# RetNet block and squared-ReLU FFN on one core: chunks 11 to 39 turned off TensorE, w_out converted by pairs of pieces from block 1 on

## The chip, the cores and the metric

One core of a Trainium2 chip runs the whole kernel. Its engines work side by side, each through its own queue in order: TensorE (PE, and PEld for its weight loads), VectorE (DVE), ScalarE (ACT), GpSimd (POOL) and the queue on SyncE (SP) that issues nearly all DMAs. The metric is the time of one execution on the device in microseconds, as the median of several runs.

## The reference

Eight heads of retention over 8 sequences of 576 tokens, then an FFN over all 4608 tokens:

```python
scores = scale * np.matmul(q, k.transpose(0, 1, 3, 2))
Dmat = np.where(rel >= 0, gamma[:, None, None] ** rel[None, :, :], 0.0)
ret = scores * Dmat[None, :, :, :]
attn = np.matmul(ret, v).astype(np.float32)          # (8, 8, 576, 64)
x = attn.transpose(0, 2, 1, 3).reshape(4608, 512)
h = np.maximum(x @ w_in, 0.0)                        # w_in 512 x 2048
out = (h * h @ w_out).astype(np.float32)             # w_out 2048 x 512
```

q, k and v are float32. The two weights reach the kernel as 64-bit words (float64), so it converts them to float32 itself with integer operations.

## The kernel before

**Phases.** In the first phase the kernel computes the retention and, interleaved with it, g = relu(x w_in)^2. In the second phase it multiplies g by w_out. Both products are done by the Strassen-Winograd scheme of seven products (`PRODUCTS`), the sums of quarters being made on VectorE. g goes to DRAM (`g_dram`) in five of its seven forms (`G_KEPT`); the other two, S2 and S4, are made in the second phase by `made`, from forms that have come back. This is the same in both kernels.

**Retention.** There are 40 chunks: four of 128 tokens and a half one of 64 for each sequence (chunks 4, 9, 14 and so on are half). For each chunk q and k must be turned, so that the head's dimension lies on partitions. `turn` (L406) does it on TensorE: sixteen small matmuls against an identity (eight for a half chunk) into PSUM (L414), and two copies out, k by ScalarE (L417) and q by VectorE (L418). The second way is `flip` and `spread`: two VectorE transposes of 32x32 blocks (L392), one for k and one for q, and sixteen ScalarE copies of 32x256 slices, eight for a half chunk (L403), which `move` issues a few at a time. Before the change chunks 0 to 10 and 19 to 39 are turned by TensorE, and chunks 11 to 18 in the second way. `scores` multiplies k by q (L435) and masks the product on VectorE (L443). `retain_a`, `retain_b` and `retain_c` sum up the chunk before: the products within the chunk (L457), the state's growth (L460) and the state's part (L492). A small ScalarE copy of x_ps (L495) is written at the end of `retain_b`, and since it reads the PSUM tile that L457 of `retain_c` writes next, TensorE waits for it. The result is copied into xT by ScalarE (L514).

**xT.** A block is 512 tokens; there are nine. `xT[n]` holds block n's input until its steps are done. Two rooms are in `room`; block 2 has a third one in W[6], and a rule in `retain_c` (L511) issues what is left of an old block before its room is overwritten.

**Steps.** The FFN's input side is a list of steps. Block 0 has 16 of its own kind (L578) while w_in is being converted; each of blocks 1 to 8 has 28 steps, 4 pairs of row blocks (mp) times 7 products (j), of eight 128x256 matmuls each (L614). j = 0 is followed by a ScalarE copy (L624), j = 1 and 2 by a VectorE add each (L626, L628), j = 3 by a ScalarE activation (L630) and a square on POOL (L631), and j = 4, 5 and 6 by a VectorE add and a square each (L633, L637, L640, L621). PSUM has three banks for them. One iteration of the main loop (L739) handles one chunk: `retain_a`, `turn`, `move`, some steps (`ffn(.., 0)`, the first half), `retain_b`, `scores`, `retain_c`, and steps again (`ffn(.., 1)`, the second half). `PACE` says how many steps must be done by which token, so the order is fixed when the kernel is built.

**w_out.** The weights of the second phase are converted in 16 pieces of 128x512 words. A piece takes five parts (`w_out_parts`): `one` and `two` on VectorE (L210, L214), with `two` two ScalarE activations (L218, L219, together `beside`), then `three`, `four` and `five` on VectorE (L222, L225, L228), `three` needing the activations. After every second piece come two parts of sums (L245 to L248), after every fourth eight more and two stores to DRAM. With three fetches in front these are 139 parts. A step of a block issues one part at most: before the change 13 of them in the first steps of block 1, and one in every step from block 3 on. `held` keeps a part with activations out of the last step of a first half. The pieces arrive by DMA through the SP queue in three rooms, and the fetch of piece j+3 is issued by the last part of piece j. Its staging area is W[5] and the beginning of W[6].

Of the kernel before, what the change touches and what calls it, by code (L numbers as in the profile page):

```python
# [15 lines left out]
C = 128  # L16
# [24 lines left out]
def kernel(  # L41
# [152 lines left out]
    def fetch_w(j):  # L194
        if j < len(pieces) and wide:
            nc.sync.dma_start(raw_of(j).bitcast(I64).rearrange("p (c f) -> p c f", c=N_DM), piece_src(j))
# [53 lines left out]
    def w_out_parts():  # L250

        for j in range(N_W1, N_W1 + 3):
            yield lambda j=j: fetch_w(j)
        for j in range(N_W1, len(pieces)):
            one, two, beside, three, four, five = round_parts(j)
            yield one
            yield two, beside
            yield three
            yield four

            def last(j=j, five=five):
                five()
                fetch_w(j + 3)

            yield last
            wi, m, e = pieces[j]
            mh, mq = divmod(m, N_MQ)
            if e == 1:

                at = slice(2 * mh, 2 * mh + 2)  # L270
                b = [stage[0][:, o, at, :] for o in range(4)] + [stage[1][:, o, at, :] for o in range(3)]
                r1, r2, r3, r4 = right_sums(*b)
                yield lambda r1=r1, r2=r2: (r1(), r2())
                yield lambda r3=r3, r4=r4: (r3(), r4())
            if e == 1 and mh == 1:

                for st_, at in ((stage[0], slice(0, 4)), (stage[1], slice(4, 7))):
                    yield from right_sums(*(st_[:, :, o, :] for o in range(NP)))
                    yield lambda st_=st_, at=at, mq=mq: nc.sync.dma_start(
                        w2_dram[at, :, mq, :].rearrange("o p f -> p o f"), st_.rearrange("p o s f -> p o (s f)"))  # L280
# [63 lines left out]

    st = {i: {} for i in range(N_CH)}
    u_ps = [None]

    xT = {n: xT_room[n % 2 if n < 2 else (n - 3) % 2] for n in range(N_BLK)}
    xT[2] = W[6][:, 0:N_DM * TOK].rearrange("p (c t) -> p c t", c=N_DM)

# [24 lines left out]

    N_TURN, N_BACK = 11, 19  # L380
    moves = []

    def new_qk(i):
        t = work3.tile([128, 2, HP, C], F32, tag="qk", name="qk")
        st[i]["qT"], st[i]["kT"] = t[:, 0, :, :], t[:, 1, :, :]
        return t

    def flip(i):
        cs = chunks[i][3]
        t = st[i]["flip"] = work2.tile([128, 4, 2, HP, 32], F32, tag="flip", name="flip")  # L390
        for j in (1, 0):
            nc.vector.transpose(t[:cs, :, j, :, :], loaded[i][j][:cs].rearrange("s (p e) (d a) -> s (e d) p a", e=2, d=2))  # L392

    def spread(i):
        t, to = st[i]["flip"], new_qk(i)
        for b in range(chunks[i][3] // 32):
            for g in range(4):
                moves.append((i, to[32 * g:32 * g + 32, :, :, 32 * b:32 * b + 32], t[32 * b:32 * b + 32, g, :, :, :]))

    def move(count, i=N_CH):  # L400

        while moves and count and moves[0][0] <= i:
            nc.scalar.copy(*moves.pop(0)[1:])  # L403
            count -= 1

    def turn(i):  # L406
# [90 lines left out]
    def retain_c(i):  # L497

        b_, ci, c0, cs = chunks[i]
        own, grow = within(i, 0)  # L500
        more = ci + 1 < NCH
        for j in range(0, len(own), 2):
            for f in own[j:j + 2] + (grow[j:j + 2] if more else []):
                f()
        tok = b_ * S + c0
        at = tok
        p = xp[0][:, :, 0:256].rearrange("p a (g t) -> p a g t", g=2)
        while at < tok + cs:
            n = at // TOK

            while steps and steps[0][0] <= (n - 2 if n > 4 else n - 3):  # L511
                step()
            end = min(tok + cs, (n + 1) * TOK)
            nc.scalar.copy(xT[n][:, :, at - n * TOK:end - n * TOK].rearrange("p (a g) t -> p a g t", a=2),  # L514
                           p[:, :, :, at - tok:end - tok])
            if more and at == tok:
                grown(i, 1)
            at = end
            if n_next[0] < N_BLK and (n_next[0] + 1) * TOK <= at:
                steps.extend(block_steps(n_next[0]))  # L520
                n_next[0] += 1
        st[i] = loaded[i] = None
# [76 lines left out]
    def ffn_in(n, mp, j):  # L599

        if j == 0 and mp == 0:

            if n not in sums_x:
                sums_x[n] = sum_x(n)
            for f in sums_x[n]:
                f()
        left, right, to = PRODUCTS[j]
        if j in OPENS:
            sums[to] = ps_f.tile([128, 2, HT], F32, tag="f", name=f"h_{to}")
        p = sums[to]  # L610
        for mm in range(2):
            w = w_in[mp][:, mm, WI_SLOT[left], :, :]
            for c in range(2):
                nc.tensor.matmul(p[:, mm, :], lhsT=w[:, c, :], rhs=xs[n][right][:, c, :],  # L614
                                 start=(j in OPENS and mm == 0 and c == 0), stop=(j in CLOSES and c == 1),
                                 skip_group_check=True)
        g = g_of(mp)
        p1, u2, p15 = (p_room[mp % 2][:, s, :, :] for s in range(3))

        def square(t):  # L620
            nc.vector.scalar_tensor_tensor(t, t, 0.0, t, op0=ALU.max, op1=ALU.mult)  # L621

        if j == 0:
            nc.scalar.copy(p1, p)  # L624
        elif j == 1:
            nc.vector.tensor_tensor(u2, p, p1, op=ALU.add)  # L626
        elif j == 2:
            nc.vector.tensor_tensor(p15, p, p1, op=ALU.add)  # L628
        elif j == 3:
            nc.scalar.activation(g["A11"], p, AF.Relu)  # L630
            nc.gpsimd.tensor_tensor(g["A11"], g["A11"], g["A11"], op=ALU.mult)  # L631
        elif j == 4:
            nc.vector.tensor_tensor(g["A22"], p, p15, op=ALU.add)  # L633
            square(g["A22"])
        elif j == 5:

            nc.vector.tensor_tensor(g["S3"], p, u2, op=ALU.add)  # L637
            square(g["S3"])
        else:
            nc.vector.tensor_tensor(g["A12"], p, p1, op=ALU.add)  # L640
            square(g["A12"])
            queue.extend(g_sums(n, mp))

        if mp == N_MP - 1 and j in (3, 4, 5) and n_next[0] > n + 1:
            if n + 1 not in sums_x:
                sums_x[n + 1] = sum_x(n + 1)
            sums_x[n + 1].pop(0)()
        if j in (6, 0, 1, 2, 3):
            some(2 if n == 1 and mp == 0 else 1)
        if n == 1 and 1 <= j < 5 and mp + 1 < N_MP:  # L650
            sums_w.setdefault(mp + 1, sum_w_in(mp + 1)).pop(0)()

        if n >= 3 or n_w2[0] < 3 + 2 * 5:
            if not (held[0] and type(w_out_next[0]) is tuple):
                n_w2[0] += 1
                f = w_out_next[0]
                w_out_next[0] = next(w_out_steps, None)
                for f in f if type(f) is tuple else (f,):
                    f and f()
            if n == N_BLK - 2 and (mp, j) in ((2, 3), (3, 3)):  # L660
                assert w_out_next[0] is None
                fetch_w2(mp - 2)
# [34 lines left out]
    def ffn(i, half):  # L697

        gone[0] += chunks[max(0, min(i, N_CH - 1))][3] / 2
        if steps and steps[0][0] == 0:  # L700

            move(6)
            for f in (step, lambda: convert(6)) if half else (lambda: convert(6), step):
                f()
            if half and steps and steps[0][0] == 0:
                step()
                convert(6)
            return
        if not behind:
            behind.append((gone[0] - HALF, done[0]))  # L710
        points = behind + [p for p in PACE if p[0] > behind[0][0]]
        want = points[-1][1]
        for (x0, y0), (x1, y1) in zip(points, points[1:]):
            if gone[0] < x1:
                want = y0 + (y1 - y0) * (gone[0] - x0) / (x1 - x0)
                break
        count = max(1, int(want) - done[0])
        while steps and count:
            held[0] = half == 0 and count == 1
            move(3)  # L720
            step()
            count -= 1
        held[0] = False
# [15 lines left out]
    for i in range(N_CH + 1):  # L739
# [42 lines left out]
        else:  # L782
            if i == N_EARLY + 1:
                gone[0] = TOK
            retain_a(i - 1)
            if i < N_TURN or N_BACK <= i < N_CH:
                turn(i)
            move(C, i)
            ffn(i - 1, 0)
# [1 line left out]
            if i < N_CH:  # L791
                scores(i)
            retain_c(i - 1)
            if N_TURN <= i + 1 < N_BACK:
                spread(i + 1)
            if N_TURN <= i + 2 < N_BACK:
                flip(i + 2)
            ffn(i - 1, 1)
        if i == 0:
# [267 lines left out]
```

## Time and profile before

| what | value |
|---|---|
| median of 7 runs | 985.08 us (984.05 to 986.17) |
| profiled execution, its own time | 985.45 us |
| profiled execution, span from first to last instruction | 983.6 us |
| mean granted TensorE clock | 0.998 |
| first phase, block 0 begins its last step | 102.4 us |
| first phase, retention of the last chunk | about 529 us |
| second phase begins | about 585 us |
| DMA | 181.46 MB, mean 184 GB/s |

| stretch, us | PE busy | DVE busy | ACT busy | POOL busy |
|---|---|---|---|---|
| 0 to 101.8 | 93.0 | 74.9 | 45.4 | 26.9 |
| 101.8 to 230 | 127.9 | 96.2 | 74.1 | 31.5 |
| 230 to 515 | 282.8 | 223.7 | 73.3 | 60.8 |
| 515 to 584.7 | 69.3 | 44.2 | 8.1 | 7.5 |
| 584.7 to 983.6 | 395.2 | 321.0 | 33.4 | 0.0 |

In the prediction's extracts a line of the timeline gives the start in us, the length in us, the engine (a "q" behind it means the engine's sequencer), the line of the kernel, the operation, the tile written and the tiles read, the number of instructions run together, and in brackets the idle time before and what ended it. A line of the groups gives busy time, mean duration in ns, and idle time before with its releaser. [...]

### The profile page before, as it was taken

To read this page: it belongs to the slowest core of one execution; us is meant where nothing else is said; L and a number is where in the kernel's file an instruction comes from. 1 tells how busy PE (TensorE), PEld (TensorE's weight loads), DVE (VectorE), ACT (ScalarE), POOL (GpSimd) and SP (SyncE) were. 2 spreads that over 40 slices of the span, in tenths; PEclk is the share of its full clock that TensorE was granted. 3 is DMA by queue.
4 is the path that set the end of the run, shared out by engine and by line. 5 is a ranking of instruction groups with operands and counts; after the bars stand their busy time and mean duration, and the time that the engine had idled before them with its cause. 6 is when DMAs were issued, how large, how long until landed. Compare 5 with 4: busy or idle time off the path is not lost.

```text
span 983.6 us, 24277 instructions
## 1 busy us (share of the span) xinstructions
PE 968.1 (98%) x10404; PEld 864.1 (88%) x10404; DVE 760.0 (77%) x1426; ACT 234.2 (24%) x573; POOL 126.7 (13%) x121
## 2 busy tenths in 40 slices
PE   7899999999999999999999999999999999999998
PEld 6645788888888888888888899999999999999998
DVE  3889798648777877878776577878888788787876
ACT  3554474752223222312211010000000000000000
POOL 3221222311213221221201000000000000000000
PEclk9999999999999999999999999999999999999999
DMA  8985665643756676585348966645352544534241
GB/s 201 244 224 151 178 189 138 175 141 90 259 188 192 163 276 191 162 285 144 127 182 303 355 247 239 225 162 196 109 204 109 182 180 165 208 124 172 86 172 44
DMA packets 172012, 181.46 MB, mean 184 GB/s; under 512 B 118144, under 2 KB 132480, under 8 KB 165248
## 3 DMA queue, kind: packets, MB, share of 16 engines
q1 hardware_dynamic: 169792, 179.38, 56.4%
q8 instruction: 82, 1.34, 0.6%
q10 hardware_dynamic: 2112, 0.52, 0.3%
q14 instruction: 26, 0.21, 0.1%
HBM read 109.36 MB, written 70.52 MB: 183 GB/s over the span
## 4 chain that ended last, share of the span: by engine, by line
PE 87%; DVE 8%; DMA 2%; ACT 1%; issue 1%; SPq 0%; DVEq 0%; ACTq 0%
PE o_b L916 16%; PE h_b L614 15%; PE o_a L916 11%; PE o_c L916 11%; PE h_a L614 10%; PE h_c L614 10%; PE h_ps L578 4%; PE x_ps L457 3%; PE sc_ps L435 2%; PE x_ps L492 2%; PE t_ps L414 2%; DMA g<-g_dram 1%; DVE room L621 1%; DVE w L222 1%; DVE w L225 1%
## 5 line engine op out<-in xcount | busy, mean ns | idle before, releaser
L614 PE MATMUL h_b<-room,w 128*128 128x256 f32 x736 | 177.2, 384 | 1.2 <-DVE room L541 1.0
L614 PEld LDWEIGHTS h_b<-room,w 128*128 128x128 f32 x736 | 137.4, 190 | 21.2 <-PE t_ps L414 1.1
L916 PE MATMUL o_b<-w,room 128*128 128x128 f32 x1168 | 144.4, 276 | 0.2 <-DVE room L868 0.2
L916 PEld LDWEIGHTS o_b<-w,room 128*128 128x128 f32 x1168 | 137.3, 192 | 0.4 <-DVE room L868 0.4
L916 PE MATMUL o_c<-w,room 128*128 128x128 f32 x1008 | 123.0, 275 | 0.0
L916 PEld LDWEIGHTS o_c<-w,room 128*128 128x128 f32 x1008 | 117.7, 192 | 0.0
L614 PE MATMUL h_c<-room,w 128*128 128x256 f32 x480 | 114.4, 381 | 0.0
L614 PE MATMUL h_a<-room,w 128*128 128x256 f32 x448 | 107.5, 383 | 0.0
L614 PEld LDWEIGHTS h_c<-room,w 128*128 128x128 f32 x480 | 90.7, 190 | 12.3
L614 PEld LDWEIGHTS h_a<-room,w 128*128 128x128 f32 x448 | 84.0, 190 | 11.6
L916 PE MATMUL o_a<-w,a 128*128 128x128 f32 x688 | 85.7, 276 | 0.0
L916 PEld LDWEIGHTS o_a<-w,a 128*128 128x128 f32 x688 | 81.2, 192 | 0.1
L631 POOL TENSOR_TENSOR room<-room 128x512 f32<-128x512 f32 x32 | 34.0, 1061 | 365.9 <-ACT room L630 295.1
L930 ACT COPY r<-o_a 128x128 f32<-128x128 f32 x53 | 14.2, 267 | 272.5 <-PE o_a L916 236.8
L621 DVE SCALAR_TENSOR_TENSOR room<-room 128x512 f32<-128x512 f32 x96 | 70.3, 732 | 3.3
L633 DVE TENSOR_TENSOR room<-h_b,room 128x512 f32<-128x512 f32 x32 | 22.1, 690 | 50.9 <-PE h_b L614 47.4
L578 PE MATMUL h_ps<-room,w 128*128 128x512 f32 (+1 forms) x152 | 59.8, 542 | 1.5 <-DVE w L228 0.8
L375 POOL TENSOR_TENSOR q_ld<-q_ld,dv 128x512 f32<-128x512 f32 (+1 forms) x39 | 47.2, 1211 | 75.2 <-DMA q_ld<-in_q_dram 64.5
L457 PEld LDWEIGHTS x_ps<-qk,v_ld 64*64 64x64 f32 x1152 | 40.5, 137 | 13.8 <-issue 11.8
L457 PE MATMUL x_ps<-qk,v_ld 64*64 64x64 f32 x1152 | 49.9, 227 | 1.4 <-ACT u_sb L495 1.3
L578 PEld LDWEIGHTS h_ps<-room,w 128*128 128x128 f32 x152 | 28.3, 195 | 24.4 <-issue 20.5
L403 ACT COPY qk<-flip 32x256 f32<-32x256 f32 x120 | 48.3, 402 | 1.7
(115 smaller groups left out, 1435.2 us busy)
## 6 DMA issues: line engine op xcount, KB each, us to landing
g_dram<-room SPq DMA_DIRECT2D x32, 1280.0 KB, 5.8
a<-g_dram SPq DMA_DIRECT2D x30, 1024.0 KB, 6.0
room<-g_dram SPq DMA_DIRECT2D x15, 1024.0 KB, 6.3
w<-w_dram SPq DMA_DIRECT2D x7, 1792.0 KB, 10.6
out_dram<-room SPq DMA_DIRECT2D x17, 512.0 KB, 3.3
w<-in_moe_w_in_dram SPq DMA_DIRECT2D x16, 512.0 KB, 5.7
w<-in_moe_w_out_dram SPq DMA_DIRECT2D x16, 512.0 KB, 5.2
v_ld<-in_v_dram SPq DMA_DIRECT2D x31, 256.0 KB, 3.5
```

Source lines behind the costliest of these rows:

```text
L375: engine.tensor_tensor(t, t, dv[:cs, :, NCH + ci:NCH + ci + 1].to_broadcast([cs, H, D]), op=ALU.mult)
L403: nc.scalar.copy(*moves.pop(0)[1:])
L414: nc.tensor.transpose(p[:, h, j, hp, :], loaded[i][j][rows(h), 2 * hp:2 * hp + 2, :], ident[rows(h), rows(h)])
L435: nc.tensor.matmul(sc[e][rows(h), hp, :], lhsT=kT[rows(e), hp, t], rhs=qT[rows(e), hp, t], start=True, stop=True, skip_group_check=True)
L457: own.append(lambda hp=hp, e=e, b=b: nc.tensor.matmul(x_at(hp, b, h), lhsT=s["vs"][rows(h), 2 * hp + b, :], rhs=s["ret"][rows(h), e, hp, : ...
L492: nc.tensor.matmul(x_at(hp, b, h), lhsT=u[rows(e), hp, :], rhs=s["qT"][rows(e), hp, CH * h:CH * h + CH], start=clears(b, hp // 2), stop=Fa ...
L578: nc.tensor.matmul(p.rearrange("p h t -> p (h t)"), lhsT=w[:, c, :], rhs=xT[0][:, c, lo * HT:hi * HT], start=(c == 0), stop=(c == N_DM - 1))
L614: nc.tensor.matmul(p[:, mm, :], lhsT=w[:, c, :], rhs=xs[n][right][:, c, :], start=(j in OPENS and mm == 0 and c == 0), stop=(j in CLOSES a ...
L621: nc.vector.scalar_tensor_tensor(t, t, 0.0, t, op0=ALU.max, op1=ALU.mult)
L631: nc.gpsimd.tensor_tensor(g["A11"], g["A11"], g["A11"], op=ALU.mult)
L633: nc.vector.tensor_tensor(g["A22"], p, p15, op=ALU.add)
L916: nc.tensor.matmul(p, lhsT=s["lefts"][left][:, m, :], rhs=w_out[j][:, m, WO_SLOT[right], :], start=(i in OPENS and m == 0), stop=(i in CLO ...
```

## The change

- `w_out_parts` handles two pieces together: `one`, `two` with `beside` for the first and the second piece, then `three`, `four`, `five` for the first and for the second.
- A part of w_out is issued by a step while fewer than 0.8 x (steps done since block 0) have been issued. So the conversion begins with block 1 and ends early in block 7.
- All blocks use the two rooms for xT by turns; block 2 no longer lies in W[6]. The rule at L511 is the same for all blocks.
- `N_BACK` is gone: every chunk from 11 on goes by `flip`. `spread` is merged into it. The two transposes become two entries of a list `flips`, of which `ffn` issues one before each step. The slices carry the number of steps at which they become due, three after the second transpose, and `move` issues none before that unless it is called with C, as it is at the start of an iteration for the chunk that is needed next.

```diff
--- before.py
+++ after.py
@@ -251,18 +251,21 @@
 
         for j in range(N_W1, N_W1 + 3):
             yield lambda j=j: fetch_w(j)
-        for j in range(N_W1, len(pieces)):
-            one, two, beside, three, four, five = round_parts(j)
-            yield one
-            yield two, beside
-            yield three
-            yield four
-
-            def last(j=j, five=five):
-                five()
-                fetch_w(j + 3)
-
-            yield last
+        for j in range(N_W1 + 1, len(pieces), 2):
+
+            pair = [round_parts(j - 1), round_parts(j)]
+            for one, two, beside, *_ in pair:
+                yield one
+                yield two, beside
+            for i, (_, _, _, three, four, five) in zip((j - 1, j), pair):
+                yield three
+                yield four
+
+                def last(i=i, five=five):
+                    five()
+                    fetch_w(i + 3)
+
+                yield last
             wi, m, e = pieces[j]
             mh, mq = divmod(m, N_MQ)
             if e == 1:
@@ -344,9 +347,7 @@
 
     st = {i: {} for i in range(N_CH)}
     u_ps = [None]
-
-    xT = {n: xT_room[n % 2 if n < 2 else (n - 3) % 2] for n in range(N_BLK)}
-    xT[2] = W[6][:, 0:N_DM * TOK].rearrange("p (c t) -> p c t", c=N_DM)
+    xT = {n: xT_room[1 - n % 2] for n in range(N_BLK)}
 
 
 
@@ -377,7 +378,7 @@
 
 
 
-    N_TURN, N_BACK = 11, 19
+    N_TURN = 11
     moves = []
 
     def new_qk(i):
@@ -385,22 +386,29 @@
         st[i]["qT"], st[i]["kT"] = t[:, 0, :, :], t[:, 1, :, :]
         return t
 
+    flips = []
+
     def flip(i):
         cs = chunks[i][3]
-        t = st[i]["flip"] = work2.tile([128, 4, 2, HP, 32], F32, tag="flip", name="flip")
-        for j in (1, 0):
+        t = work2.tile([128, 4, 2, HP, 32], F32, tag="flip", name="flip")
+
+        def one(j):
             nc.vector.transpose(t[:cs, :, j, :, :], loaded[i][j][:cs].rearrange("s (p e) (d a) -> s (e d) p a", e=2, d=2))
 
-    def spread(i):
-        t, to = st[i]["flip"], new_qk(i)
-        for b in range(chunks[i][3] // 32):
-            for g in range(4):
-                moves.append((i, to[32 * g:32 * g + 32, :, :, 32 * b:32 * b + 32], t[32 * b:32 * b + 32, g, :, :, :]))
+        def two():
+            one(0)
+            to = new_qk(i)
+            for b in range(cs // 32):
+                for g in range(4):
+
+                    moves.append((i, done[0] + 3, to[32 * g:32 * g + 32, :, :, 32 * b:32 * b + 32], t[32 * b:32 * b + 32, g, :, :, :]))
+
+        flips.extend([lambda: one(1), two])
 
     def move(count, i=N_CH):
 
-        while moves and count and moves[0][0] <= i:
-            nc.scalar.copy(*moves.pop(0)[1:])
+        while moves and count and moves[0][0] <= i and (moves[0][1] <= done[0] or count == C):
+            nc.scalar.copy(*moves.pop(0)[2:])
             count -= 1
 
     def turn(i):
@@ -508,7 +516,7 @@
         while at < tok + cs:
             n = at // TOK
 
-            while steps and steps[0][0] <= (n - 2 if n > 4 else n - 3):
+            while steps and steps[0][0] <= n - 2:
                 step()
             end = min(tok + cs, (n + 1) * TOK)
             nc.scalar.copy(xT[n][:, :, at - n * TOK:end - n * TOK].rearrange("p (a g) t -> p a g t", a=2),
@@ -650,7 +658,7 @@
         if n == 1 and 1 <= j < 5 and mp + 1 < N_MP:
             sums_w.setdefault(mp + 1, sum_w_in(mp + 1)).pop(0)()
 
-        if n >= 3 or n_w2[0] < 3 + 2 * 5:
+        if n_w2[0] < 0.8 * (done[0] - N_0):
             if not (held[0] and type(w_out_next[0]) is tuple):
                 n_w2[0] += 1
                 f = w_out_next[0]
@@ -718,6 +726,9 @@
         while steps and count:
             held[0] = half == 0 and count == 1
             move(3)
+            for f in flips[:1]:
+                f()
+            del flips[:1]
             step()
             count -= 1
         held[0] = False
@@ -783,7 +794,7 @@
             if i == N_EARLY + 1:
                 gone[0] = TOK
             retain_a(i - 1)
-            if i < N_TURN or N_BACK <= i < N_CH:
+            if i < N_TURN:
                 turn(i)
             move(C, i)
             ffn(i - 1, 0)
@@ -791,9 +802,7 @@
             if i < N_CH:
                 scores(i)
             retain_c(i - 1)
-            if N_TURN <= i + 1 < N_BACK:
-                spread(i + 1)
-            if N_TURN <= i + 2 < N_BACK:
+            if N_TURN <= i + 2 < N_CH:
                 flip(i + 2)
             ffn(i - 1, 1)
         if i == 0:
```

## The prediction

> **What bounds the kernel now.** I read the busy table first, then the waits of the matrix engine, then its weight loads in order of time around a turn, then the loads of the other engines by stretch.
>
> ```profile
> PE 968.1 (98%) x10404; PEld 864.1 (88%) x10404; DVE 760.0 (77%) x1426; ACT 234.2 (24%) x573; POOL 126.7 (13%) x121
> ```
>
> TensorE is busy 98% of the span, and its longest listed wait for another engine in the stretch from 230 to 535 us is 1.1 us. In the first phase one step of a block (eight 128x256 matmuls) goes out every 1.72 us with hardly a break, so an instruction taken off TensorE's queue there shortens the kernel by its place in the queue, not by its latency. That place is read from the weight loads. The first two views are a chunk that TensorE turns, and one of the chunks (11 to 18) that VectorE and ScalarE turn already:
>
> ```profile
> 407.54 0.14 PEld L460 LDWEIGHTS u_ps<-v_ld,k_ld 64*64 64x64 f32 x2
> 407.75 0.32 PEld L414 LDWEIGHTS t_ps<-w,k_ld 64*128 64x128 f32 x8
> 408.00 0.33 PEld L414 LDWEIGHTS t_ps<-w,q_ld 64*128 64x128 f32 x8
> 408.39 0.73 PEld L614 LDWEIGHTS h_b<-room,w 128*128 128x128 f32 x4
> ```
>
> ```profile
> 160.63 0.14 PEld L460 LDWEIGHTS u_ps<-v_ld,k_ld 64*64 64x64 f32 x2
> 160.84 0.30 PEld L614 LDWEIGHTS h_b<-room,w 128*128 128x128 f32 x2
> ```
>
> After the last L460, the next step's weights follow in 0.21 us without a turn and in 0.85 us with one: a turn holds TensorE for 0.64 us (407.75 to 408.39), though its sixteen matmuls are listed at 223 ns each.
>
> ScalarE has room; VectorE has it in most places, but not at the beginning of block 1:
>
> ```profile
> 110.00:130.00 20.00, 20.00 (x251) 17.07 (x250) 17.85 (x28) 12.94 (x32) 4.11 (x3) 1.00 0.75 230
> 130.00:150.00 20.00, 19.81 (x236) 16.50 (x236) 19.72 (x28) 15.19 (x36) 7.93 (x6) 1.00 0.70 187
> ...
> 170.00:190.00 20.00, 20.00 (x209) 17.02 (x211) 12.22 (x19) 15.84 (x40) 5.07 (x4) 1.00 0.72 203
> ```
>
> The columns are stretch, length, then PE, PEld, DVE, ACT and POOL busy. From 130 to 150 VectorE works 19.7 of 20 us. ScalarE, carrying the slices of chunks 11 to 18, stands at 13 to 16 of 20. Between 230 and 515 it is busy only 73 of 285 us.
>
> **What goes.** Chunks 19 to 39 lose their turn: 21 x 0.64 = 13.4 us of TensorE's queue (half chunks show 0.64 too). Four of the 21 turns (chunks 20, 25, 30, 35) come when the chunk before is a half one and L476 returns at once, so they stand alone between two runs of steps. A run of three steps takes 5.38 us, one of four 7.10: beyond 1.72 a step each run costs 0.21. Merging four pairs of runs gives 4 x 0.2 = 0.8 us. And two waits of the scores for L418's copy out of PSUM, 0.9 and 0.3 (1.1 listed from 230 to 535), have no cause any more. Sum: 13.4 + 0.8 + 1.1 = **15.3 us**. Beyond 585 us (the second phase, 399 us) nothing changes: its `made` sums stand in both kernels.
>
> **What comes on ScalarE.** Sixteen full and five half chunks bring 16x16 + 5x8 = 296 slices (L403):
>
> ```profile
> L403 ACT COPY qk<-flip x120: 400/402/405, 114.3 to 214.7; 32x256 f32<-32x256 f32 x120
> ```
>
> 296 x 0.402 = 119 us, less 21 copies L417 of 0.54 = 11. So 73 + 108 = 181 of some 270 us: two thirds, which is hidden on average. It isn't hidden at one place per chunk. L495, a tiny copy of x_ps, stands in ScalarE's queue behind the first half's steps, and TensorE's retain_c (L457) waits for it. Normally it starts 0.34 us after the last weights of L492 and costs nothing; here is what happens when ScalarE is late:
>
> ```profile
> 484.37 0.72 ACT L218 ACTIVATE w<-w,exp_bias 128x512 uint32<-128x512 uint32 x1 [4.36 <-DVE w L210]
> 485.00 0.68 ACT L219 ACTIVATE w<-w 128x512 f32<-128x512 uint32 x1
> 485.57 0.57 ACT L630 ACTIVATE room<-h_a 128x512 f32<-128x512 f32 x1
> 486.05 0.14 ACT L495 COPY u_sb<-x_ps 128x2 f32<-128x2 f32 x1
> ```
>
> TensorE stood 0.53 us there. Before the change the slices of a chunk were issued in the half after retain_c and the rest at the start of the next iteration, so ScalarE was clear again by L495. Now a chunk's slices become due three steps after its second transpose and trickle, three before each step, through first halves as well; and the two activations of a w_out piece (1.39 together) fall among them. Carrying ScalarE's queue through the written order with these durations, at 1.72 a step: in iteration 11 (the ten last slices 4.0, p1 copy 0.59, activations 1.39, three slices 1.2, against three steps) it is late by some 2 us; in iterations 20 and 27, where activations fall in with slices just ahead of L495, by 1.5 each; in 32, 24 and 26 by 0.5 and less. Sum **6 us**. Bounds: 0, since in 102 to 215 us the same slices delayed L495 by at most 0.12; and 29 chunks x 0.53 = 15.4.
>
> **What comes on VectorE.** 42 transposes less 21 copies:
>
> ```profile
> L392 DVE STREAM_TRANSPOSE flip<-k_ld 128x512 f32<-128x512 f32 (+1 forms) x8 | 5.6, 698 | 0.0
> L392 DVE STREAM_TRANSPOSE flip<-q_ld 128x512 f32<-128x512 f32 (+1 forms) x8 | 5.3, 665 | 0.0
> ```
>
> 21 x 1.36 - 13.1 (L418) = +15.5 us over 285 us in which VectorE is busy 224; and a part of w_out's conversion leaves that stretch. All 16 pieces cost some 80 us of VectorE (L210 to L228 2.9 a piece, the right sums 34 in all). Before, 13 of the 139 parts run in block 1, none in block 2, and the rest from block 3 on. At 0.8 a step 22 run in each of blocks 1 and 2: some 19 us move into 102 to 230 us, where VectorE is busy 96 of 128. The average holds. Summing by iteration, VectorE's written work runs ahead of TensorE's by up to 3.5 us around iteration 12 (4/5 part a step, w_in's sums of 0.8, the flips, five PSUM adds and three squares of 0.7 per seven steps) and by 2 until iteration 15; before, the same sum peaked at 2.9 at iteration 11 and was paid off at once, for a few tenths of TensorE waiting. Two adds in each seven steps (L633, L640) have one step of 1.72 us before TensorE needs their bank. I take **2.5 us**; bounds 0 (the first 13 steps have fewer parts than before) and 8 (3.5 plus some 4.5 that VectorE loses between 110 and 150 us where single instructions take 1.4 to 1.5 in place of 0.69). Doing both bit operations of a pair before its two `three`s sets them two steps or more behind the activations; the 0.4 us that L222 waited for L219 after 215 us is worth nothing on TensorE.
>
> **What moves.** The w_out steps take their DMAs along: 16 fetches of 512 KB (5.2 us to land) and eight stores (6.7 and 7.4), on the one queue that also loads q, k, v. The first fetch goes behind block 0's last store, which before held that queue until 111 us, and VectorE's first part comes three steps (5.2 us) later: up to 2 us of VectorE waiting at a place where it idled for TensorE before (1.6 us from 110 to 118), taken at 0 and inside the bound of 8. Later fetches have eight parts or more to land. The transposes need q scaled by POOL one iteration earlier than a turn did. Measured against the time at which chunk i-3's L495 ran, the scaling of chunks 19 to 39 ended 1.8 us (chunk 37) to 15.6 us before its flip would start, and q is the second of the two: 0. With two rooms for xT the last step of block 0 is drawn ahead of chunk 8's copy, and the last three or so of block 2 ahead of chunk 17's: the same matmuls in another order, hidden since TensorE has them to do anyway. But three steps of block 1 then come an iteration earlier, so that chunk 10, the last one turned, has one step less between its turn and its scores: the case of the 0.9 us above, **0.5 us**, between 0 and 1.
>
> **Sum.** -15.3 + 6 + 2.5 + 0.5 = -6.3 us. The profiled execution's own time is 985.45 (span 983.6), 0.37 over the median of 985.08: 979.15, or **978.8** as a median.
>
> [...] By the rows the new way is indeed dearer in engine time: 1.36 + 6.4 against 0.64 + 0.59 + 0.69 a chunk. If all of that counted, 21 x 5.8 would make it 1107 us; the row that TensorE alone sets the pace makes the 0.64 count.
>
> **Rivals.** *Both queues keep up.* The flip stage before shows no loss at L495 and hardly a wait for VectorE. Then only the 0.5 is lost and maybe another: 985.1 - 15.3 + 1 = **971**. Against it: w_out's activations were almost absent from that stage. *ScalarE takes it all back.* The 0.53 us seen at 486 comes at each of 29 chunks: 15.4, **985**, no change. Against it: two thirds load, and the last step of a first half still withholds the activations. *VectorE becomes the bound, slower.* Its lag of block 1 isn't paid off, because blocks 2 to 7 now run at 80 to 100% of TensorE's time with some 4% more where POOL is active; then L633 and L640, two in seven steps, each hold TensorE by an add of 0.69. Blocks 1 to 7 have 56 such places, 38.6 us; from 23 of them on (23 x 0.69 = 15.9, against 15.3 - 0.5) the change loses; at 30 places, nothing else lost, it is 985.1 - 14.8 + 20.7 = **991**. For it: 19.7 of 20 us at 130; against: 12 of 20 at 170, and iterations 32 and 36 before had VectorE sums at 0.96 to 1.0 of TensorE's without a wait of TensorE.
>
> **How the numbers follow.** A measurement of this kernel tells 0.2% (2 us) from no change. Forecast 0.53 (its own range 974 to 983); queues keep up 0.26; ScalarE takes it back 0.10; VectorE bound 0.11. So faster 0.79, same 0.10, slower 0.11. The range takes in the clean case but for its lower end, and reaches to no change: 969.5 to 985.
>
> **What would show it.** Right: no L414 after some 112 us, the step run after L460 in 0.21; ScalarE 110 us busier; TensorE's waits list holding L457 <- ACT L495 with some 6 us in a handful of places, and L614 <- DVE with 2 to 3 us between 110 and 190. Wrong: L495 late at most chunks, VectorE over 98% in 150 to 230, or a flip waiting for POOL. If L457's wait is near 0.5 us in all, the first rival holds.

## The result, and the profile after

The changed kernel takes 989.87 us (median of 18 runs, 985.58 to 994.13), the kernel before 985.22 (42 runs): a ratio of 1.0046, 95% interval 1.0037 to 1.0055. By the medians the change loses 4.65 us where 6.3 were forecast as a gain. The profiled execution has a span of 990.0 us. It is 1.9 us slower than the median of the 18, and its mean granted clock, 0.986, is the lowest of them (their median is 0.991), so what is read below as lost to the clock is rather the upper end.

From the page of the changed kernel, the busy times, and the granted TensorE clock in 40 slices of the span (tenths of full speed):

```profile
PE 961.5 (97%) x10108; PEld 856.1 (86%) x10108; DVE 782.9 (79%) x1447; ACT 342.1 (35%) x848; POOL 127.9 (13%) x121
...
PEclk7999989999999999999999999999999999999999
```

The same clock row before the change:

```profile
PEclk9999999999999999999999999999999999999999
```

TensorE has 296 matmuls fewer, as the change says. The clock row has an 8 in the slice around 130 us, where the row of before has a 9. The 7 at its very beginning lies ahead of the place where the change sets in. Line numbers moved by 8 or 9: L495, the tiny copy, is now L503, L457 is L465, L403 is L411 and L614 is L622.

The gain is there. This is the place between a chunk's last growth matmul and the next step, for a chunk that TensorE turned before (weight loads of the changed kernel in order of time):

```profile
410.84 0.14 PEld L468 LDWEIGHTS u_ps<-v_ld,k_ld 64*64 64x64 f32 x2
411.05 0.30 PEld L622 LDWEIGHTS h_a<-room,w 128*128 128x128 f32 x2
```

0.21 us, as predicted. But TensorE's waits in the stretch from 100 to 540 us are no longer small (who waited for whom, total, times, longest):

```profile
PE x_ps L465 <- ACT u_sb L503: 7.9, 5, 3.0
PE h_b L622 <- DVE room L641: 2.7, 2, 1.6
PE h_b L622 <- DVE room L549: 2.2, 1, 2.2
PE x_ps L465 <- POOL v_ld L453: 1.5, 1, 1.5
```

**Where the time went.** I took the start of every group of weight loads in both traces and subtracted what the group takes undisturbed (1.724 us a step, 0.21 a run of steps, 0.55 the scores, 0.62 `retain_c`). What is left over between 100 and 540 us is 3.9 us before and 24.4 after. The run of steps that ends the first phase begins at 529.57 us before and at 536.84 after, 7.3 later. That is, within 0.2, 20.5 of new waiting, less 13.4 for the turns and 0.8 for the merged runs, plus 0.8 by which this execution was already late at 101 us, before the change sets in. The 24.4 us, place by place (the time is that of the group or run of steps in which TensorE lost; the wait itself can lie up to 6 us later):

| at, us | lost on TensorE, us | what was late |
|---|---|---|
| 116 | 1.6 | GpSimd: L453, the scaling of v, behind the late q of chunk 12 |
| 127 | 3.2 | ScalarE, ahead of L503 |
| 131 to 138 | 3.0 | half clock for 6.8 us |
| 155, 189, 238 | 1.9, 1.0, 0.5 | VectorE |
| 259 | 2.8 | ScalarE, ahead of L503 |
| 264 | 1.7 | half clock for 3.4 us |
| 301 | 2.2 | VectorE: L549, a sum for the next block |
| 305 | 1.7 | half clock for 3.4 us |
| 344, 357 | 0.7, 1.5 | ScalarE, ahead of L503 |
| 434 | 2.1 | VectorE |

ScalarE 8.2, VectorE 7.7, GpSimd 1.6, the clock 6.4; the rest is under 0.6 us.

The largest place, in order of time. First ScalarE in the changed kernel, then TensorE's weight loads beside it:

```profile
122.53 4.15 ACT L411 COPY qk<-flip 32x256 f32<-32x256 f32 x10
126.70 0.58 ACT L632 COPY room<-h_a 128x512 f32<-128x512 f32 x1
128.68 0.72 ACT L218 ACTIVATE w<-w,exp_bias 128x512 uint32<-128x512 uint32 x1 [1.39 <-DVE w L210]
129.31 0.65 ACT L219 ACTIVATE w<-w 128x512 f32<-128x512 uint32 x1
129.86 1.22 ACT L411 COPY qk<-flip 32x256 f32<-32x256 f32 x3
131.10 0.16 ACT L503 COPY u_sb<-x_ps 128x2 f32<-128x2 f32 x1
```

```profile
127.59 0.56 PEld L443 LDWEIGHTS sc_ps<-qk 64*64 64x64 f32 x32
131.32 0.19 PEld L465 LDWEIGHTS x_ps<-qk,v_ld 64*64 64x64 f32 x2 [3.16 <-ACT u_sb L503]
132.38 2.63 PEld L622 LDWEIGHTS h_c<-room,w 128*128 128x128 f32 x7
```

The tiny copy could have run at about 127.9: L500's weights begin at 127.36, and at an undisturbed chunk, 409.63, the copy begins 0.58 us behind them. It stands behind ten slices, a copy out of PSUM, two activations and three slices more, and the activations were 1.39 us late themselves, since VectorE had not yet made their input. TensorE stood 3.16 us, and when it went on, seven weight loads took 2.63 us, at a granted clock of 0.50, where eight take 1.59 at full clock (at 121.98 us).

By stretches (length, then PE, PEld, DVE, ACT and POOL busy, clock, DMA) the changed kernel shows it too:

```profile
110.00:130.00 20.00, 16.78 (x218) 13.68 (x216) 15.28 (x24) 11.49 (x27) 5.61 (x5) 1.00 0.81 211
130.00:150.00 20.00, 18.68 (x218) 15.64 (x219) 14.54 (x23) 12.87 (x33) 3.57 (x3) 0.83 0.40 112
150.00:170.00 20.00, 18.41 (x201) 15.51 (x200) 18.77 (x31) 11.84 (x27) 4.17 (x3) 1.00 0.70 197
170.00:190.00 20.00, 20.00 (x250) 17.06 (x249) 19.19 (x28) 11.24 (x28) 7.69 (x6) 1.00 0.61 173
```

TensorE is busy 16.8 of 20 us from 110 on, where it was busy all 20 before, and from 130 to 150 its granted clock is 0.83.

### The profile page after: what moved, and what is told of

Read it like the earlier page. It is cut to its first block, busy times and chain, and to the rows that moved or that the text cites. A ratio compares the mean times of both kernels' runs of the same rounds, so it can differ in the third digit from the quotient of the medians.

```text
span 990.0 us, 24023 instructions
## 1 busy us (share of the span) xinstructions
PE 961.5 (97%) x10108; PEld 856.1 (86%) x10108; DVE 782.9 (79%) x1447; ACT 342.1 (35%) x848; POOL 127.9 (13%) x121
## 5 line engine op out<-in xcount | busy, mean ns | idle before, releaser
L622 PE MATMUL h_b<-room,w 128*128 128x256 f32 x768 | 186.2, 385 | 5.4 <-DVE room L641 2.7
L411 ACT COPY qk<-flip 32x256 f32<-32x256 f32 x416 | 167.4, 402 | 6.0
L622 PEld LDWEIGHTS h_b<-room,w 128*128 128x128 f32 x768 | 143.6, 190 | 27.1 <-DVE room L641 3.5
L622 PE MATMUL h_c<-room,w 128*128 128x256 f32 x512 | 126.1, 390 | 0.1
L622 PE MATMUL h_a<-room,w 128*128 128x256 f32 x512 | 123.3, 384 | 0.0
L622 PEld LDWEIGHTS h_c<-room,w 128*128 128x128 f32 x512 | 99.2, 196 | 15.1 <-DVE room L636 0.5
L622 PEld LDWEIGHTS h_a<-room,w 128*128 128x128 f32 x512 | 96.8, 191 | 14.3 <-issue 0.5
L629 DVE SCALAR_TENSOR_TENSOR room<-room 128x512 f32<-128x512 f32 x96 | 72.3, 753 | 3.3
L465 PEld LDWEIGHTS x_ps<-qk,v_ld 64*64 64x64 f32 x1152 | 40.7, 138 | 24.3 <-issue 14.5
L465 PE MATMUL x_ps<-qk,v_ld 64*64 64x64 f32 x1152 | 50.1, 227 | 11.1 <-ACT u_sb L503 8.5
L641 DVE TENSOR_TENSOR room<-h_b,room 128x512 f32<-128x512 f32 x32 | 22.0, 688 | 48.5 <-PE h_b L622 48.4
L376 POOL TENSOR_TENSOR q_ld<-q_ld,dv 128x512 f32<-128x512 f32 (+1 forms) x39 | 44.6, 1144 | 90.8 <-DMA q_ld<-in_q_dram 70.7
```

The source lines that it names most:

```text
L376: engine.tensor_tensor(t, t, dv[:cs, :, NCH + ci:NCH + ci + 1].to_broadcast([cs, H, D]), op=ALU.mult)
L411: nc.scalar.copy(*moves.pop(0)[2:])
L465: own.append(lambda hp=hp, e=e, b=b: nc.tensor.matmul(x_at(hp, b, h), lhsT=s["vs"][rows(h), 2 * hp + b, :], rhs=s["ret"][rows(h), e, hp, : ...
```

## The experiments

Theory A was formed from this trace: the losses are ScalarE's lateness at the tiny copy, VectorE's load of blocks 1 and 2 (the late load of chunk 12 was counted here), and a clock that drops behind long waits. Times are medians; each set of four ran beside the kernel before (985.35, 984.96 and 984.85 us).

**1. The turns alone.** In the kernel before:

```diff
-    N_TURN, N_BACK = 11, 19
+    N_TURN, N_BACK = 11, N_CH
```

> The kernel before with one number changed: chunks 19 to 39 are turned by VectorE and ScalarE too, in the old way (both transposes at once, slices in the second half and in a burst); w_out and xT as before. Theory A (the loss lies in ScalarE's queue ahead of the tiny copy of x_ps, in VectorE's load of block 1 and 2, and in the clock that drops after long waits): 21 x 0.64 + 0.8 + 1.1 gained, some 6 us of ScalarE's lateness at chunks 25 to 37 lost, none of the losses of blocks 1 and 2: 975 to 981. Rival B (all of the loss comes from moving w_out's conversion forward): 970 to 973. Rival C (turning on VectorE and ScalarE is itself the loss): 987 or more.

982.96 us, ratio 0.9976 (0.9966 to 0.9986). Turning off TensorE pays by itself, so rival C falls; but the gain is less than theory A had. Its trace has some 16 us left over in place of 3.9: with the old order ScalarE, or VectorE at a block's beginning, is late in several places by 1.2 to 2.2 us (247, 286, 316, 418, 453 and 483 us), and the clock drops twice, 1.7 us each.

**2. The conversion of w_out alone.** In the changed kernel:

```diff
-    N_TURN = 11
+    N_TURN, N_BACK = 11, 19
...
-            if i < N_TURN:
+            if i < N_TURN or N_BACK <= i < N_CH:
                 turn(i)
...
-            if N_TURN <= i + 2 < N_CH:
+            if N_TURN <= i + 2 < N_BACK:
                 flip(i + 2)
```

> The changed kernel, but chunks 19 to 39 are turned by TensorE again; w_out by pairs from block 1 on, xT in two rooms, chunks 11 to 18 with the new trickle. Theory A: the losses of blocks 1 and 2 alone (119 to 195 us of the changed kernel: 1.6 + 3.2 + 1.9 + 1.0, and 3 of the clock), without the gain: 993 to 998. Rival B: 1000 or more, since the whole of 20 us of waits would stay without the 14 us gained. Rival C: 984 to 987.

994.55 us, ratio 1.0098 (1.0083 to 1.0113). The other half of the change (with the new order of chunks 11 to 18's slices) costs 9 us without the gain. The same places are lost as in the changed kernel: 1.6 at 116, 3.6 at 128 and 1.7 of half clock behind it, 1.9 at 155 and 1.0 at 189 us.

**3. First halves kept free of activations.** In the changed kernel:

```diff
-            held[0] = half == 0 and count == 1
-            move(3)
+            held[0] = half == 0
+            if half or count > 1:
+                move(3)
```

> The changed kernel, but no part with activations is issued in any first half, and no slices before the last step of a first half. Theory A: TensorE's waits for the tiny copy of x_ps (8 us in the changed kernel, of which 3.2 at 127 and 2.8 at 259) fall to some 2, and with them the two clock drops behind them (some 5 us): 977 to 981. Rival (VectorE's load is the loss, and ScalarE waits only because it is fed late): 987 to 990.

The edit also keeps slices out of a first half until its last step. 987.34 us, ratio 1.0030 (1.0018 to 1.0042): theory A missed, and the time lies where the rival had it. The wait at 127 us goes, but VectorE is 3.6 us late for L641 at about 150 us, behind three instructions of 1.2 to 1.5 us each, with the clock at half for 6.8 us behind it. ScalarE is still 3.5 late at 256, and there it is indeed fed late: L218 waits 2.94 us for VectorE, with ten slices behind it.

**4. w_out started 8 steps later** (and at 0.85 a step in place of 0.8). In the changed kernel:

```diff
-        if n_w2[0] < 0.8 * (done[0] - N_0):
+        if n_w2[0] < 0.85 * (done[0] - N_0 - 8):
```

> The changed kernel, but w_out's conversion starts 8 steps later (0.85 a step): the first fetches go behind the loads of chunk 12. Theory A: VectorE's wait of 3.1 us for k of chunk 12 goes (1.6 us on TensorE), and the activations leave iteration 11, where ScalarE was 3.2 us late and the clock fell for 6.8 us: 981 to 984. Rival (only the sum of the work counts, not where it starts): 988 to 991.

981.89 us, ratio 0.9968 (0.9955 to 0.9981), as theory A had it. 13.4 us are left over, nothing is lost at 116 us, and the clock doesn't drop (its mean is 1.000 over the profiled execution).

**5. Only the late loads of chunk 12.** In the changed kernel they go ahead of iteration 9's second half:

```diff
             retain_c(i - 1)
...
+            if i == 9:
+                load(i + 3)
             ffn(i - 1, 1)
...
-            load(i + 3)
+            if i != 9:
+                load(i + 3)
```

> The changed kernel, but the loads of chunk 12 are issued ahead of the second half of iteration 9, so ahead of block 0's last store and of w_out's first fetches. Theory A: VectorE's wait of 3.1 us at 119 us goes and with it 1.6 us of TensorE; the lateness of ScalarE at 127 us stays: 987.5 to 989. Rival (the wait at 119 us was the root of the one at 127 us): 983 to 986.

986.55 us, ratio 1.0015 (1.0005 to 1.0026): 3.3 us better than the change, between the two expectations. The 1.6 us at 116 go. The wait for ScalarE stays, at 2.5 instead of 3.2 us, and in the profiled execution no clock drop followed it. What was late shows on VectorE, on GpSimd and on TensorE in the changed kernel:

```profile
119.39 0.71 DVE L396 STREAM_TRANSPOSE flip<-k_ld 128x512 f32<-128x512 f32 x1 [3.09 <-DMA k_ld<-in_k_dram]
```

```profile
118.23 1.06 POOL L376 TENSOR_TENSOR q_ld<-q_ld,dv 128x512 f32<-128x512 f32 x1 [16.32 <-PE h_b L622]
119.25 1.04 POOL L639 TENSOR_TENSOR room<-room 128x512 f32<-128x512 f32 x1
120.25 1.06 POOL L453 TENSOR_TENSOR v_ld<-v_ld,dv 128x512 f32<-128x512 f32 x1
```

```profile
121.36 0.14 PEld L465 LDWEIGHTS x_ps<-qk,v_ld 64*64 64x64 f32 x2 [1.91 <-POOL v_ld L453]
```

The three steps of block 1 drawn into iteration 9 issue block 0's last store and three fetches of w_out on the same queue, ahead of those loads. TensorE's wait ended with GpSimd and not with VectorE, unlike what the expectations of experiments 4 and 5 say: GpSimd scales q of chunk 12 (L376) ahead of v of chunk 10 (L453), the loads of q were issued from 110.9 us on, and the scaling began only at 118.23 (the line names a matmul as what ended its wait; the last of the three loads of q came in at 118.1). Before the change the same scaling began at 101.90, and with this experiment's edit at 101.95. VectorE's own wait for k ended at 119.39, and the add behind it at 120.68, while L453 ended at 121.31 and TensorE went on at 121.36.

**6. The start and the hold, together and apart.** Starting 24 steps after block 0 (at 0.95 a step), and holding activations back in a first half while slices are still to come:

```diff
-        if n_w2[0] < 0.8 * (done[0] - N_0):
+        if n_w2[0] < 0.95 * (done[0] - N_0 - 24):
...
-            held[0] = half == 0 and count == 1
+            held[0] = half == 0 and (count == 1 or len(moves) > 0)
```

> The changed kernel, but w_out's conversion starts 24 steps after block 0 (0.95 a step), and in a first half no part with activations is issued while slices of a turn are still to come. Theory A: what block 1 and 2 lost goes altogether, and ScalarE is late by little afterwards; what stays is VectorE's lateness at the beginning of some blocks (2 to 5 us): 976 to 980. Rival (a later start makes the conversion denser, and that loses as much again): 982 or more.

977.53 us, ratio 0.9923 (0.9909 to 0.9937): as theory A had it. The first edit without the second:

> The start at 24 steps (0.95 a step) alone, without holding activations back while slices are to come. Theory A: ScalarE's queue carried through this order is late by 7 us in all (iterations 17, 20, 22, 26, 28) where it was late by 1 with the hold, with two or so clock drops: 983 to 987. Rival (the start alone brought the gain, the hold nothing): 977 to 979.

983.80 us, ratio 0.9989 (0.9979 to 1.0000). ScalarE is late at L503 by 1 to 2.6 us in five places. The second edit without the first, at the change's own 0.8:

> The changed kernel with the hold alone; the conversion starts with block 1 as in the change. Theory A: the wait for ScalarE at 127 us (ten slices, then activations) shrinks and those at 259 and 357 us nearly go, VectorE's losses of block 1 and 2 stay: 983 to 987. Rival (hold and start each bring the same gain, since they cure the same waits): 978 to 981.

989.05 us, ratio 1.0043 (1.0030 to 1.0056): a miss. Against the change's 989.87 the start gains 6.1 us, the hold 0.8, both 12.3. With the hold alone the wait at 127 us falls from 3.2 to 0.7 us and the one at 357 from 1.5 to 0.2, but VectorE is 2.7 us late at 150 where it was 1.9, and the place at 259 grows from 2.8 to 3.5. Why that place grows is seen on ScalarE:

```profile
254.32 0.73 ACT L218 ACTIVATE w<-w,exp_bias 128x512 uint32<-128x512 uint32 x1 [3.05 <-DVE w L210]
254.95 0.67 ACT L219 ACTIVATE w<-w 128x512 f32<-128x512 uint32 x1
255.65 4.15 ACT L411 COPY qk<-flip 32x256 f32<-32x256 f32 x10
259.83 0.60 ACT L638 ACTIVATE room<-h_a 128x512 f32<-128x512 f32 x1
260.32 0.16 ACT L503 COPY u_sb<-x_ps 128x2 f32<-128x2 f32 x1
```

The activations are issued in the second half before, as the hold wants it, but VectorE is late with their input, and ScalarE idles 3.05 us in front of them with ten slices behind. At this place VectorE's backlog turns into ScalarE's.

**7. Does a long wait cost more than its length?** In the kernel before, needless copies of x_ps into a spare place of `room` are written ahead of the tiny copy; nobody reads the place. Nine copies at each of five chunks; or, with `1 <= ci <= 3` and `range(3)` in these lines, three at each of fifteen:

```diff
+        if 10 <= i < 35 and ci == 2:
+            for _ in range(9):
+                nc.scalar.copy(room[:, 5120:5376], xp[0][:, 0, :])
         nc.scalar.copy(u_sb[(2 * ci + (cs // CH)) % 3][:, 0:2, 0:1], xp[0][:, :, cs - CH:cs - CH + 1])
```

> The kernel before with nine needless ScalarE copies of x_ps (0.37 us each) ahead of the tiny copy, at chunks 12, 17, 22, 27 and 32; their target is read by nobody. Theory A (the tiny copy sets when TensorE goes on, and a long wait lowers its clock): five waits of 3.3 us and a drop of 3.4 or 6.8 us of half clock behind most of them: 985.2 + 16.5 + some 6 = 1005 to 1010, and the granted clock shows the drops. Rival (the waits are hidden, or the drops had another cause): 985 to 990, or 1002 with no drop.

> The kernel before with the same 45 needless copies, but three at each of 15 chunks. Theory A: 15 waits of 1.1 us and no drop of the clock: 985.2 + 16 = 1000 to 1003. Rival (the clock counts the sum of waits): as much as with five long waits.

Five long waits: 1014.19 us, ratio 1.0291 (1.0276 to 1.0307). Fifteen short ones: 1001.18 us, ratio 1.0160 (1.0144 to 1.0176). The same 45 copies cost 29 us or 16. TensorE's weight loads around one long wait, and one short wait, each in its own kernel:

```profile
153.85 0.56 PEld L435 LDWEIGHTS sc_ps<-qk 64*64 64x64 f32 x32
157.86 0.18 PEld L457 LDWEIGHTS x_ps<-qk,v_ld 64*64 64x64 f32 x2 [3.46 <-ACT u_sb L498]
158.93 3.06 PEld L617 LDWEIGHTS h_b<-room,w 128*128 128x128 f32 x8
162.08 2.46 PEld L617 LDWEIGHTS h_c<-room,w 128*128 128x128 f32 x8
```

```profile
141.05 0.56 PEld L435 LDWEIGHTS sc_ps<-qk 64*64 64x64 f32 x32
142.65 0.14 PEld L457 LDWEIGHTS x_ps<-qk,v_ld 64*64 64x64 f32 x2 [1.03 <-ACT u_sb L498]
143.27 1.59 PEld L617 LDWEIGHTS h_b<-room,w 128*128 128x128 f32 x8
```

Behind 3.46 us of waiting eight weight loads take 3.06 us (the granted clock is 0.60 from 158 to 165 us), behind 1.03 they take 1.59, as in the kernel before at 303.94 us. The sums nearly close: 5 x 3.46 plus 10.2 us lost to half clock (drops of 6.8, 6.8, 3.4, 3.4 and 3.4 us) is 27.5 of the 29; 15 x 1.03 is 15.5 of the 16, with no drop in the stretch from 100 to 540 us. The expectation of 1005 to 1010 was too low, since all five drops came and two were double.

**8. What is left.** On top of the start and the hold, at the last step of a block the next block's first two sums ahead of the step's own add:

```diff
+        if mp == N_MP - 1 and j == 6 and n_next[0] > n + 1:
+            if n + 1 not in sums_x:
+                sums_x[n + 1] = sum_x(n + 1)
+            while len(sums_x[n + 1]) > 2:
+                sums_x[n + 1].pop(0)()
         if j == 0:
             nc.scalar.copy(p1, p)
```

> The start at 24 steps with the hold, and besides: at the last step of a block the first two sums of the next block's input (L548, L549) are made ahead of that step's own add. Theory A: the wait of 2.8 us for L549 at 290 us and the clock drop of 1.6 behind it go: 977.5 - 4 = 973 to 975. Rival (the two sums only change places with the add, for which TensorE then waits as long): 976.5 to 978.5.

975.71 us, ratio 0.9905 (0.9889 to 0.9921), just over what was expected. The wait at the beginning of block 4 falls from 2.8 to 0.5 us and no drop follows; 7.0 us are left over in all, in the fastest of this version's five executions. It has the lowest median of all versions tried, 9 us better than before. Against experiment 6 with both edits its interval overlaps (0.9909 to 0.9937 there): that the wait is gone is seen, that the 1.8 us between the medians are its gain is not clear of the noise. TensorE's waits in it are all short (its longest ones):

```profile
PE sc_ps L443 <- DVE qk L426: 3.2, 3, 1.4
PE x_ps L465 <- ACT u_sb L503: 2.7, 7, 0.5
PE h_ps L586 <- DVE w L228: 1.8, 2, 1.2
```

**9. The pairs.** The version of experiment 6 with both edits, but w_out piece by piece again:

```diff
-            for one, two, beside, *_ in pair:
+            for i, (one, two, beside, three, four, five) in zip((j - 1, j), pair):
                 yield one
                 yield two, beside
-            for i, (_, _, _, three, four, five) in zip((j - 1, j), pair):
                 yield three
```

> The start at 24 steps with the hold, but w_out piece by piece as before the change and not by pairs. If the pairs keep VectorE from waiting for the activations (each held back by up to four steps), VectorE waits 1 to 2 us at several pieces and TensorE behind it: 980 to 984. Rival (the pairs are worth nothing): 976.5 to 978.5.

979.19 us, ratio 0.9941 (0.9927 to 0.9954). The interval overlaps that of the pairs (0.9909 to 0.9937). Whether they are worth anything stays open: the medians differ by 1.7 us, between the two expectations, and the intervals rule out neither 0 nor 3 us.

## Why the prediction was wrong

The step that failed is the sum of what comes back, 6 for ScalarE, 2.5 for VectorE and 0.5 for chunk 10: 9.0 us, where the trace of the changed kernel has 24. Two terms make most of the gap. VectorE was sized at 2.5 us and cost 7.7, and the half clock behind long waits, which was no term at all, cost 6.4 in this execution. ScalarE cost 8.2 in place of 6, and GpSimd, taken at nothing, 1.6. Term by term:

- **"Sum: 13.4 + 0.8 + 1.1 = 15.3 us"** held. The turns' place is 0.21 us, 296 matmuls are gone, and the two waits of the scores for the copy out of PSUM are gone with them.
- **ScalarE, "6 us"**: the mechanism and the places were right, the size was off. Late by 3.2 and 2.8 us where 2 and 1.5 were carried (iterations 11 and 20), by 1.5 at 357 as carried (iteration 27), and 8.2 in all. The queue was carried as if the activations' inputs were ready. They were not: L218 waited 1.39 us for VectorE at 127 us and 1.19 at 252.
- **What moves, taken at 0 for the first fetch and for q's scaling**: 1.6 us. The prediction looked at VectorE waiting for the first fetch, and at the scaling of q for chunks 19 to 39. It did not look at chunk 12, whose loads were now queued behind the store and the fetches; its late q held up GpSimd, and v of chunk 10 behind it.
- **VectorE, "2.5 us"**, with a bound of 8: it was 7.7, so the bound held and the size did not. Two things made most of it. The add L641 (at 157 and 438 us) and the mask L451 (at 193), for which TensorE waited, stood behind VectorE instructions of 1.2 to 1.5 us. And the sums at a block's beginning, 1.0 us late already before, came 2.2 late at 301 us. This is VectorE in the changed kernel ahead of the add L641 at 158, and POOL beside it:

```profile
154.70 1.51 DVE L240 TENSOR_TENSOR w<-w 128x512 f32<-128x512 f32 x1
156.13 1.27 DVE L247 TENSOR_TENSOR w<-w,w 128x256 f32<-128x256 f32 x1
157.44 1.16 DVE L248 TENSOR_TENSOR w<-w,w 128x256 f32<-128x256 f32 x1
158.52 0.68 DVE L641 TENSOR_TENSOR room<-h_b,room 128x512 f32<-128x512 f32 x1
```

```profile
154.15 1.51 POOL L639 TENSOR_TENSOR room<-room 128x512 f32<-128x512 f32 x1 [11.19 <-ACT room L638]
155.62 1.50 POOL L376 TENSOR_TENSOR q_ld<-q_ld,dv 128x512 f32<-128x512 f32 x1
157.09 1.23 POOL L453 TENSOR_TENSOR v_ld<-v_ld,dv 128x512 f32<-128x512 f32 x1
```

  L247 and L248 take 0.42 us each at 441 us, where POOL is idle. Both engines are slow in the same 4 us; that the one slows the other was not tried by itself and stays open.
- **The clock was no term at all.** 6.4 us of the loss in the profiled execution. Without it the sum of this trace would have come out near no change. The profile before held a hint at most: its mean granted clock is 0.998, not 1, by one drop of 3.4 us at 22 us. But it has no wait of over 1.1 us in the stretch that mattered, and the prediction went no further.
- **The chunk-10 term, "0.5 us"**: 0.1.
- **The rivals.** None was right by itself. "VectorE becomes the bound" had the sign, and its condition, waits at L633 and L640, is seen at 155 and 434 us, but not at 23 places (nor at 22, from which on its own sum has the change lose: 22 x 0.69 = 15.2 against 14.8); two or three long waits with the clock behind them did what it wanted many short ones for. "ScalarE takes it all back" wanted 0.53 us at each of 29 chunks; the trace has a few places of 0.7 to 3.2.

The prediction also added up the two engines' lateness separately, each against its own bound. They are not separate: at 127 and at 252 us ScalarE's activations waited for VectorE, and the clock dropped behind the waits that followed. Experiment 6 fits that, with 6.1 and 0.8 us gained apart and 12.3 together; how much of the 24 us comes from this coupling was not measured.

## What to carry to other kernels

When work is taken off the engine that sets the pace and given to engines that are idle on average, look for the one instruction in each of their queues that the first engine waits for, and keep long or input-waiting work from standing in front of it. A part that is drawn forward takes its DMAs along, and delays what was loaded behind them on that queue (1.6 us of TensorE here, by way of a third engine). Here fifteen waits of 1.03 us cost about their sum, 16 us; waits of over 2 us often cost half as much again (2.8 us at 259 cost 4.5), at 127 us double, because TensorE then ran at half clock (five of 3.46 us: 29).

## What the runs showed of the hardware

In the profiled executions here, between 100 and 540 us, the granted clock fell to 0.50 for 3.4 or 6.8 us at a time; in the changed kernel from 130.8, 263.9 and 304.9 us on, with stretches of 3.16, 2.75 and 2.29 us without a weight load that ended at 131.3, 262.1 and 303.7. There are 26 places where TensorE lost 2.1 us or more to a late engine; a drop began at 19 of them, during the wait or within 2 us of its end. There was none at the places that lost under 2.0 us, some fifty of them over 1 us. The smallest loss with a drop was 2.2 us, the largest without one 3.5. In some places the loss is split into two or three waits close together, as in that one of 3.5. Counted by single stretches without a weight load, all thirteen of 2.7 us or longer had a drop, and five of the ten between 2.2 and 2.7.

One drop followed an idle stretch of 2.26 us (experiment 1, at 419 us). The wait for L549 has a drop in one execution and none in another: at 301 us in the changed kernel with one, at 297 in experiment 3 without. What decides between them was not shown, nor whether it has a part in the spread of the changed kernel's runs (8.6 us from lowest to highest). Over its 18 runs a lower mean granted clock goes with a longer time only loosely: the two fastest, 985.58 and 985.71 us, have 0.991 and 0.997, the slowest, 994.13, has 0.988.
